# Second softmax of batches 2 to 7: eight TensorE transposes replaced by VectorE block transposes and sixteen small DMAs

## The chip, the cores and the metric

The kernel runs on one core of a Trainium2 chip. The metric is the device time of one execution in microseconds (us). TensorE is called PE below, the loading of its weights PEld, VectorE DVE, ScalarE ACT and SyncE SP; SPq and ACTq are the queues on which SP and ACT issue DMAs.

## The reference, cut to what matters

```python
# x: 8 batches x 8 heads x 512 tokens x 64;  state: 8 x 8 x 32 x 64
scores = scale * x @ state.T;   a  = softmax(scores);   xread = a @ state
scores2 = scale * state @ x.T;  a2 = softmax(scores2);  sread = a2 @ x      # the part that is changed
attn = concat([xread, sread], axis=2)          # 512 + 32 rows per head
h = attn_as_rows(4352 x 512) @ w_in            # 512 -> 2048
g = where(h >= 1, h, where(h <= -1, 0, (h + 1)**2 / 4))
out = g @ w_out                                # 2048 -> 512
```

## The kernel before

All large products are made of three TensorE products of split numbers (high times high, low times high, high times low). The hidden layer of one batch is done in 8 steps j = 0 to 7. In each step `g1(b, j)` makes two hidden tiles in PSUM (L481 to L483, 12 matmuls), which ACT and DVE turn into `gh` and `gl` (`relu` L487, `square` L490, `bound` L493, `high` L502, `low` L507), and `g2` of the step before multiplies those of the previous step with w_out (L539 to L541, 24 matmuls). `bound` reads the hidden tiles last, so the next `g1` needs it: the PSUM tag `h` has two buffers.

The attention of batch b+1 is spread over the steps of batch b. A generator, `Attention.steps`, is advanced after steps 1, 3, 4 and 6, and `sw_make` (L423, L438, L442) prepares weights after steps 0, 2, 4 and 6. The four pieces of the generator are:

- after step 1: the scores `sc` (L253); DVE turns them in 32x32 blocks for the first softmax (L260) and finds the maxima for the second (L318); ACT takes the second softmax's exponentials to `e2` (L322, `exp2`).
- after step 3: the first softmax's sums and scaling, and `turn2` and `keep_turned`: eight 128x128 TensorE transposes of `e2` into the PSUM tile `e2p` (L333), one ACT copy back over `e2` (L337), and the reciprocal `r2` (L339, L340).
- after step 4: the first softmax turned back (L300) and split (L303, L306), and `read2`: 32 small products `sr` with `e2` as weights and the tokens `xn` (L353).
- after step 6: `keep2`, a transpose of the result.

Batches 0 and 1 are written in an order made by a planner (`Plan`, which has its own calls of `turn2` and `keep_turned`); batches 2 to 7 take theirs from `steps`. In that second part a scheduler of the framework orders the instructions of each engine by its own priorities and places the semaphore waits. A DMA counts on one of eight semaphores in turn (DMAHW0 to DMAHW7 in the listings); a DMA waits until the one eight before it has landed. The loads of `xt` and `xn` for the next batches stand on SPq too (L217, L222).

Of the kernel before, what the change touches and what calls it, by code (L numbers as in the profile page):

```python
# [8 lines left out]
F32 = mybir.dt.float32  # L9
# [128 lines left out]
def state_exchange_moe(  # L138
# [17 lines left out]
    nc = tc.nc  # L156
    B, P, NT, H, D = x.shape
    S = NT * P
    NS = 32
    DM = H * D  # L160
    NPR = H // 2
# [9 lines left out]
    small = ctx.enter_context(tc.tile_pool(name="small", bufs=1))  # L171
    const = ctx.enter_context(tc.tile_pool(name="const", bufs=1))
    work = ctx.enter_context(tc.tile_pool(name="work", bufs=2))
# [7 lines left out]
    def ps_h(name):  # L181
        return ps.tile([P, 512], F32, tag="h", bufs=2, name=name)

    def ps_mm(name):
        return ps.tile([P, 2, 512], F32, tag="mm", bufs=1, name=name)
# [39 lines left out]
    class Attention:  # L225
# [109 lines left out]
        def keep_turned(self):  # L335
# [3 lines left out]
            nc.vector.tensor_scalar_add(self.r2, self.sum2, 1e-9)  # L339
            nc.vector.reciprocal(out=self.r2, in_=self.r2)  # L340

        def read2(self):
            b = self.b
            xn = loaded.pop(("xn", b))
            if b < 2:
                sr = self.sr = ps_mm(f"sr{b}")
            else:
                sr = self.sr = ps_h(f"sr{b}").rearrange("p (q f) -> p q f", q=2)
            for q in range(2):
                for t in range(NT):  # L350
                    for pr in range(NPR):
                        c0 = t * P + pr * NS
                        nc.tensor.matmul(  # L353
                            sr[pr * NS:(pr + 1) * NS, q, :D], lhsT=self.e2[:, q, c0:c0 + NS],
                            rhs=xn[:, t, 2 * pr + q], start=t == 0, stop=t == NT - 1,
                        )
# [22 lines left out]
        def steps(self):  # L379
            self.scores()  # L380
            for q in range(2):
                self.turn(q)
            for q in range(2):
                self.top2(q)
            for q in range(2):
                self.exp2(q)
            yield
            for f in (self.top1, self.less1, self.exp1, self.sum1, self.inv1, self.norm1):
                for q in range(2):
                    f(q)  # L390
            self.turn2()
            self.keep_turned()
            yield
            for q in range(2):
                self.back(q)
                self.high1(q)
                self.rest(q)
            self.read2()
            self.scale2()
            yield  # L400
            self.keep2()
            self.keep()
            yield
# [406 lines left out]
    for i, (b, j) in enumerate(steps):  # L810
        if j == 0:
            if b + 1 < B:
                loaded["xt", b + 1] = load_xt(b + 1)
                loaded["xn", b + 1] = load_xn(b + 1)
                att = Attention(b + 1).steps()
            elif b == B:
                sh, sl = (work.tile([P, NPR, B * NS], F32R, tag=t, name=f"s{t}") for t in ("ath", "atl"))
                src = srT.rearrange("p a b n -> p a (b n)")
                nc.vector.tensor_copy(sh, src)
                nc.vector.tensor_tensor(out=sl, in0=src, in1=sh.bitcast(F32), op=ALU.subtract)  # L820
                att_of[B] = (sh, sl)
        g1(b, j)
        if i + 1 < len(steps):
            splits(*steps[i + 1])
        g2(*(steps[i - 1] if i else (0, NJ - 1)))
        between_steps(b, j)
# [44 lines left out]
```

## Time and profile before

| | |
|---|---|
| runs | 666.66, 666.80 and 666.98 us, median 666.8 |
| profiled execution | span 664.4 us from the first to the last instruction; what lies around it is the other 2.4 us of the runs (no separate time of this execution is listed) |
| granted TensorE clock | 0.997 of full speed over the span |
| busy share of PE, ACT, DVE | 98%, 55%, 51% |
| one batch | 73.8 us: the scores of batch 3 start at 188.74 us, those of batch 4 at 262.55 us |

A busy PE is the union of pipelined matmuls, so the distance from the start of one matmul to the start of the next is the price of one, not its own duration: 0.227 us for the 128x512 matmuls, though each lasts 0.39 us. "Idle before" in a row is the time its engine stood still ahead of it, with the instruction that ended the wait.

### The profile page before, as it was taken

How to read it: one execution, taken by the hardware profiler on the slowest of the kernel's cores; microseconds unless marked ns; L12 is line 12 of the kernel's file. 1: busy time of each engine (PE TensorE's matmuls, PEld its weight loads, DVE VectorE, ACT ScalarE, POOL GpSimd, SP SyncE). 2: the span in 40 equal slices, each digit the busy share in tenths (PEclk: the TensorE clock that was granted, in tenths of full speed). 3: DMA queues.
4: the chain of work that ended last, by engine and by line, in shares of the span. 5: the costliest groups of instructions: out<-in, count | busy, mean ns of one | idle time of the engine just before them, and what ended most of it. 6: DMA issues, size and time to landing. Idle time of an engine off the chain costs nothing.

```text
span 664.4 us, 10294 instructions
## 1 busy us (share of the span) xinstructions
PE 653.2 (98%) x4444; PEld 515.3 (78%) x4444; DVE 339.9 (51%) x489; ACT 362.8 (55%) x462; POOL 0.8 (0%) x7
## 2 busy tenths in 40 slices
PE   6999999999999999999999999999999999999997
PEld 6777777777778777777777877777778787778895
DVE  4999953933365334833375335733384343333431
ACT  4899845644556445644555444644555455454632
POOL 0000000000000000000000000000000000000000
PEclk9899999999999999999999999999999999999999
DMA  8896101110110102110110103010100001000101
GB/s 346 350 393 273 64 1 64 63 65 0 65 64 1 64 1 78 50 65 1 64 64 1 64 1 120 7 64 1 65 1 1 1 26 39 1 1 1 63 1 32
DMA packets 11085, 43.64 MB, mean 66 GB/s; under 512 B 1312, under 2 KB 1440, under 8 KB 7968
## 3 DMA queue, kind: packets, MB, share of 16 engines
q1 hardware_dynamic: 5952, 33.75, 13.3%
q10 hardware_dynamic: 5088, 9.24, 3.7%
q8 instruction: 34, 0.56, 0.3%
q14 instruction: 11, 0.09, 0.0%
HBM read 34.08 MB, written 8.91 MB: 65 GB/s over the span
## 4 chain that ended last, share of the span: by engine, by line
PE 92%; ACT 4%; DVE 2%; DMA 1%; issue 0%; ACTq 0%; SPq 0%
PE acc L539 18%; PE acc L541 18%; PE acc L540 18%; PE h L481 11%; PE h L482 9%; PE h L483 9%; PE sw L423 5%; DMA xt<-in_xt_dram 1%; PE sr L353 1%; PE sc L253 1%; PE e2p L333 1%; PE warmed L198 1%; ACT u L487 1%; ACT raw_i L593 1%; ACT gh L502 0%; ACT raw_o L593 0%
## 5 line engine op out<-in xcount | busy, mean ns | idle before, releaser
L539 PE MATMUL acc<-wo,gh 128*128 128x512 f32 x544 | 213.3, 392 | 0.0
L541 PE MATMUL acc<-wo,gl 128*128 128x512 f32 x544 | 211.8, 389 | 0.0
L540 PE MATMUL acc<-wo,gh 128*128 128x512 f32 x544 | 211.7, 389 | 0.0
L493 DVE SCALAR_TENSOR_TENSOR u<-u,h 128x512 f32<-128x512 f32 x136 | 87.4, 683 | 170.5 <-ACT u L490 170.2
L487 ACT ACTIVATE u<-h,half 128x512 f32<-128x512 f32 x136 | 93.7, 690 | 146.5 <-PE h L483 145.8
L539 PEld LDWEIGHTS acc<-wo,gh 128*128 128x128 f32 x544 | 102.2, 188 | 24.6 <-issue 3.7
L541 PEld LDWEIGHTS acc<-wo,gl 128*128 128x128 f32 x544 | 102.1, 188 | 21.6
L540 PEld LDWEIGHTS acc<-wo,gh 128*128 128x128 f32 x544 | 102.2, 188 | 20.8
L507 DVE TENSOR_TENSOR gl<-u,gh 128x1024 fp32r<-128x1024 f32 x68 | 83.2, 1223 | 60.8 <-ACT gh L502 60.8
L502 ACT CAST gh<-u 128x1024 fp32r<-128x1024 f32 x68 | 71.5, 1052 | 67.0 <-DVE u L493 67.0
L490 ACT ACTIVATE u<-u 128x1024 f32<-128x1024 f32 x68 | 72.3, 1064 | 1.6
L423 PE MATMUL sw<-w,sb 64*32 64x256 f32 x1024 | 35.9, 383 | 2.2 <-DVE w L601 2.2
L423 PEld LDWEIGHTS sw<-w,sb 64*32 64x32 f32 x1024 | 15.1, 106 | 18.2 <-issue 11.3
L554 ACT COPY o<-acc 128x512 f32<-128x512 f32 x33 | 18.9, 583 | 12.0 <-PE acc L541 12.0
L481 PE MATMUL h<-ath,sw_4h 128*128 128x512 f32 x60 | 25.3, 422 | 0.1
L481 PE MATMUL h<-ath,sw_2h 128*128 128x512 f32 x60 | 24.9, 415 | 0.0
L481 PE MATMUL h<-ath,sw_0h 128*128 128x512 f32 x60 | 24.4, 410 | 0.0
L481 PE MATMUL h<-ath,sw_6h 128*128 128x512 f32 x60 | 23.9, 398 | 0.0
L483 PE MATMUL h<-atl,sw_4h 128*128 128x512 f32 x60 | 23.5, 392 | 0.0
L482 PE MATMUL h<-ath,sw_4l 128*128 128x512 f32 x60 | 23.5, 391 | 0.0
L483 PE MATMUL h<-atl,sw_6h 128*128 128x512 f32 x60 | 23.5, 391 | 0.0
L482 PE MATMUL h<-ath,sw_0l 128*128 128x512 f32 x60 | 23.5, 391 | 0.0
(173 smaller groups left out, 733.3 us busy)
## 6 DMA issues: line engine op xcount, KB each, us to landing
raw_i<-in_moe_w_in_dram SPq DMA_DIRECT2D x8, 1024.0 KB, 6.5
raw_o<-in_moe_w_out_dram SPq DMA_DIRECT2D x8, 1024.0 KB, 8.6
xn<-in_x_dram SPq DMA_DIRECT2D x8, 1024.0 KB, 4.7
out_dram<-o ACTq DMA_DIRECT2D x32, 256.0 KB, 2.0
xt<-in_xt_dram SPq DMA_DIRECT2D x15, 512.0 KB, 4.5
xt<-in_xt_dram ACTq DMA_DIRECT2D x1, 512.0 KB, 7.8
sb<-in_state_dram SPq DMA_DIRECT2D x1, 448.0 KB, 12.0
out_dram<-o SPq DMA_DIRECT2D x4, 64.0 KB, 1.7
```

The lines of the kernel that those rows point to most:

```text
L423: nc.tensor.matmul(pt[pr * NS:(pr + 1) * NS, hh, i * CI:(i + 1) * CI], lhsT=sb[rows, b, pr], rhs=w32[c + i][rows, pr], start=True, stop=True,)
L481: nc.tensor.matmul(o, lhsT=wh[:, k, sl], rhs=ah[:, k], start=first, stop=False)
L482: nc.tensor.matmul(o, lhsT=wl[:, k, sl], rhs=ah[:, k], start=False, stop=False)
L483: nc.tensor.matmul(o, lhsT=wh[:, k, sl], rhs=al[:, k], start=False, stop=last)
L487: nc.scalar.activation(out=self.u[:, i], in_=self.hs[i], func=AF.Relu, scale=0.5, bias=half)
L490: nc.scalar.activation(out=self.u, in_=self.u, func=AF.Square)
L493: nc.vector.scalar_tensor_tensor(out=self.u[:, i], in0=self.u[:, i], scalar=1.0, in1=self.hs[i], op0=ALU.min, op1=ALU.max,)
L502: nc.scalar.copy(out=gh, in_=self.u)
L507: nc.vector.tensor_tensor(out=gl, in0=self.u, in1=gh.bitcast(F32), op=ALU.subtract)
L539: nc.tensor.matmul(a, lhsT=lh, rhs=oh, start=f == 0, stop=False)
L540: nc.tensor.matmul(a, lhsT=lh, rhs=ol, start=False, stop=False)
L541: nc.tensor.matmul(a, lhsT=ll, rhs=oh, start=False, stop=f == NF - 1)
```

## The change

In `steps`, which rules batches 2 to 7, the two calls `turn2` and `keep_turned` after step 3 are gone. After step 1, behind `exp2`, two calls of `turn_blocks` make DVE transpose `e2` in 32x32 blocks into a new SBUF tile `eb`, and `shuffle` issues sixteen DMAs on SPq that put the blocks where the 128x128 transposes would have put them, back in `e2`. Each DMA moves a block of 32 partitions x 8 runs of 32 numbers (128 bytes a run, 32 KB in all). `eb` takes one of the two buffers of the tag `tmp`, in turn with `zt`. `r2` is computed in `shuffle`.

```diff
+        def turn_blocks(self, q):
+            if q == 0:
+                self.blocks = work.tile([P, 2, S], F32, tag="tmp", name=f"eb{self.b}")
+            nc.vector.transpose(out=self.blocks[:, q], in_=self.e2[:, q])
+
+        def shuffle(self):
+            b = self.b
+            self.r2 = small.tile([P, 2], F32, tag="r2", name=f"r2_{b}")
+            nc.vector.tensor_scalar_add(self.r2, self.sum2, 1e-9)
+            nc.vector.reciprocal(out=self.r2, in_=self.r2)
+            src, dst = (
+                v.rearrange("p q (t r n) -> p (q t) r n", r=NPR, n=NS) for v in (self.blocks, self.e2)
+            )
+            for r in range(NPR):
+                for pr in range(NPR):
+                    nc.sync.dma_start(
+                        out=dst[r * NS:(r + 1) * NS, :, pr], in_=src[pr * NS:(pr + 1) * NS, :, r]
+                    )
+
@@ steps
             for q in range(2):
                 self.exp2(q)
+            for q in range(2):
+                self.turn_blocks(q)
+            self.shuffle()
             yield
             for f in (self.top1, self.less1, self.exp1, self.sum1, self.inv1, self.norm1):
                 for q in range(2):
                     f(q)
-            self.turn2()
-            self.keep_turned()
             yield
```

The new lines stand ahead of most of the kernel, so a line of before from L342 on is 19 or 20 higher after: `read2`'s L353 becomes L372, `bound`'s L493 becomes L513. In the listings a number behind a name is the batch, and for `h`, `u`, `gl`, `gh` and `sw` the batch and the step.

TensorE, at the end of step 3 in the loop of batch 2 (attention of batch 3), before:

```order
L541 MATMUL acc2_3_1663<-wo2_482,gl2_2_1732 128x512
L333 MATMUL e2p3_1842<-ident_73,e2_3_1702 128x128 [waits DVE_49]
L333 MATMUL e2p3_1842<-ident_73,e2_3_1702 128x128 x7
L481 MATMUL h2_4_0_1856<-ath2_973,sw2_4h_1776 128x512 [waits DVE_49]
L482 MATMUL h2_4_0_1856<-ath2_973,sw2_4l_1777 128x512
```

and after:

```order
L560 MATMUL acc2_3_1672<-wo2_482,gh2_2_1762 128x512
L561 MATMUL acc2_3_1672<-wo2_482,gl2_2_1763 128x512
L501 MATMUL h2_4_0_1874<-ath2_973,sw2_4h_1807 128x512 [waits DVE_49]
L502 MATMUL h2_4_0_1874<-ath2_973,sw2_4l_1808 128x512
L503 MATMUL h2_4_0_1874<-atl2_974,sw2_4h_1807 128x512
```

The eight transposes are gone and the hidden products of step 4 follow `g2` directly. One step later, at `read2`, the piece before is

```order
L423 MATMUL sw2_6_1903<-w32_6_93,sb_85 32x256 x7
L423 MATMUL sw2_6_1903<-w32_7_94,sb_85 32x256 x8
L353 MATMUL sr3_1931<-xn3_1554,e2_3_1702 32x64 [waits DMAHW1_49,DVE_49]
L353 MATMUL sr3_1931<-xn3_1554,e2_3_1702 32x64 x31
L481 MATMUL h2_5_0_1967<-ath2_973,sw2_4h_1776 128x512 [waits DVE_49]
```

and after

```order
L443 MATMUL sw2_6_1921<-w32_7_94,sb_85 32x256 x8
L372 MATMUL sr3_1949<-xn3_1563,e2_3_1711 32x64 [waits DMAHW1_49,DMAHW4_49,DMAHW0_49,DVE_49]
L372 MATMUL sr3_1949<-xn3_1563,e2_3_1711 32x64 [waits DMAHW5_49,DMAHW1_49]
L372 MATMUL sr3_1949<-xn3_1563,e2_3_1711 32x64 [waits DMAHW6_49,DMAHW2_49]
L372 MATMUL sr3_1949<-xn3_1563,e2_3_1711 32x64 [waits DMAHW7_49,DMAHW3_49]
L372 MATMUL sr3_1949<-xn3_1563,e2_3_1711 32x64 x28
L501 MATMUL h2_5_0_1985<-ath2_973,sw2_4h_1807 128x512 [waits DVE_49]
```

so `read2` now waits for all eight DMA semaphores, spread over its first four products, and everything behind it on TensorE waits with it.

VectorE, after step 1 in the same loop, before:

```order
L271 TENSOR_REDUCE m1_3_1690<-z3_1689 128x16
L275 TENSOR_TENSOR z3_1689<-z3_1689,m1_3_1690 128x512 [waits DVE_49] x2
L339 TENSOR_SCALAR r2_3_1852<-sum2_3_1704 128x2 [waits Activation_49]
L340 RECIPROCAL r2_3_1852<-r2_3_1852 128x2 [waits DVE_49]
L493 SCALAR_TENSOR_TENSOR u2_2_1711<-u2_2_1711,h2_2_0_1712 128x512 [waits Activation_49]
L493 SCALAR_TENSOR_TENSOR u2_2_1711<-u2_2_1711,h2_2_1_1720 128x512
L284 TENSOR_REDUCE s1_3_1691<-z3_1689 128x16 [waits Activation_49] x2
L507 TENSOR_TENSOR gl2_2_1732<-u2_2_1711,gh2_2_1731 128x1024 [waits Activation_49]
```

and after:

```order
L271 TENSOR_REDUCE m1_3_1699<-z3_1698 128x16
L275 TENSOR_TENSOR z3_1698<-z3_1698,m1_3_1699 128x512 [waits DVE_49]
L345 STREAM_TRANSPOSE eb3_1720<-e2_3_1711 128x512 [waits Activation_49] x2
L350 TENSOR_SCALAR r2_3_1723<-sum2_3_1713 128x2
L513 SCALAR_TENSOR_TENSOR u2_2_1742<-u2_2_1742,h2_2_0_1743 128x512 [waits Activation_49]
L351 RECIPROCAL r2_3_1723<-r2_3_1723 128x2 [waits DVE_49]
L513 SCALAR_TENSOR_TENSOR u2_2_1742<-u2_2_1742,h2_2_1_1751 128x512
L275 TENSOR_TENSOR z3_1698<-z3_1698,m1_3_1699 128x512
L284 TENSOR_REDUCE s1_3_1700<-z3_1698 128x16 [waits Activation_49]
L527 TENSOR_TENSOR gl2_2_1763<-u2_2_1742,gh2_2_1762 128x1024 [waits Activation_49]
```

Both block transposes, which wait for ACT's `exp2`, stand ahead of `bound` of step 2 now, and one of the two subtractions (L275) has moved behind it.

SyncE's queue around the same place, before:

```order
L222 DMA xn3_1554<-in_x_dram 128x2048 [waits DMAHW2_49,PE_49]
L217 DMA xt4_2134<-in_xt_dram 128x1024 [waits DMAHW6_49,DMAHW7_49,DMAHW0_49,PE_49]
L217 DMA xt4_2134<-in_xt_dram 128x1024
L222 DMA xn4_2137<-in_x_dram 128x2048 [waits DMAHW1_49,PE_49]
L217 DMA xt5_2717<-in_xt_dram 128x1024 [waits DMAHW6_49,DMAHW7_49,DMAHW5_49,PE_49]
```

and after, to the tenth of the sixteen new DMAs:

```order
L217 DMA xt4_2152<-in_xt_dram 128x1024 [waits DMAHW6_49,PE_49]
L217 DMA xt4_2152<-in_xt_dram 128x1024 [waits DMAHW7_49]
L357 DMA e2_3_1711<-eb3_1720 32x8x32 [waits DMAHW3_49,DMAHW4_49,DMAHW2_49,DMAHW5_49,DMAHW0_49,DVE_49]
L357 DMA e2_3_1711<-eb3_1720 32x8x32 [waits DMAHW1_49]
L357 DMA e2_3_1711<-eb3_1720 32x8x32 [waits DMAHW2_49]
L357 DMA e2_3_1711<-eb3_1720 32x8x32 [waits DMAHW3_49]
L357 DMA e2_3_1711<-eb3_1720 32x8x32 [waits DMAHW4_49]
L357 DMA e2_3_1711<-eb3_1720 32x8x32 [waits DMAHW5_49]
L357 DMA e2_3_1711<-eb3_1720 32x8x32 [waits DMAHW6_49]
L357 DMA e2_3_1711<-eb3_1720 32x8x32 [waits DMAHW7_49]
L357 DMA e2_3_1711<-eb3_1720 32x8x32 [waits DMAHW0_49]
L357 DMA e2_3_1711<-eb3_1720 32x8x32 [waits DMAHW1_49]
```

The sixteen stand behind the load of `xt` and ahead of that of `xn`, which waits for `read2` in both versions; from the ninth on each waits for the one eight places ahead of it.

## The prediction

> **What bounds the kernel now.** I read the page's busy shares first, then the chain that ended last. The first two fields of an engine's row are its busy us and share of the span.
>
> ```profile
> span 664.4 us, 10294 instructions
> PE 653.2 (98%) x4444; PEld 515.3 (78%) x4444; DVE 339.9 (51%) x489; ACT 362.8 (55%) x462; POOL 0.8 (0%) x7
> ...
> PE 92%; ACT 4%; DVE 2%; DMA 1%; issue 0%; ACTq 0%; SPq 0%
> ```
>
> PE is busy for 653.2 of 664.4 us, and the chain is PE for 92%. So what leaves PE's instruction stream in batches 2 to 7 is time won, unless something else comes late there; what DVE, ACT or a queue gains or loses counts only where PE has to wait for it. Whether PE stands still at the changed place is in the timeline (start us, duration us, engine, line): the transposes of batch 3 with the matmuls around them, then a passage from `g2` to `g1` with nothing between, and the first and last of the six groups.
>
> ```profile
> 202.03 0.39 PE L539 MATMUL acc<-wo,gh 128*128 128x512 f32 x1
> ...
> 207.25 0.39 PE L541 MATMUL acc<-wo,gl 128*128 128x512 f32 x1
> 207.48 1.03 PE L333 MATMUL e2p<-ident,e 128*128 128x128 f32 x8
> 208.27 0.48 PE L481 MATMUL h<-ath,sw_4h 128*128 128x512 f32 x1
> 208.59 0.40 PE L482 MATMUL h<-ath,sw_4l 128*128 128x512 f32 x1
> ...
> 165.64 0.39 PE L539 MATMUL acc<-wo,gh 128*128 128x512 f32 x1
> ...
> 171.08 0.39 PE L481 MATMUL h<-ath,sw_0h 128*128 128x512 f32 x1
> 171.31 0.39 PE L482 MATMUL h<-ath,sw_0l 128*128 128x512 f32 x1
> ...
> 133.62 1.03 PE L333 MATMUL e2p<-ident,e 128*128 128x128 f32 x8
> ...
> 502.87 1.03 PE L333 MATMUL e2p<-ident,e 128*128 128x128 f32 x8
> ```
>
> PE does not wait: the transposes start 0.23 us after the last matmul, the usual distance.
>
> **The change part by part.** *Eight transposes leave PE, six times.* From the first matmul of `g2` to the second of the following `g1` it is 208.59 - 202.03 = 6.56 us with the transposes, and 171.31 - 165.64 = 5.67 us without. The difference, 0.89 us, holds the transposes and the slower start of the matmul behind them. Six batches: 5.3 us. Nothing lies beside this on PE, so all of it is on the path.
>
> *Two DVE block transposes and the moved `r2`.* The same operation on the same size stands in the groups (busy us, mean ns); the places where it can hurt are in the timelines of DVE, ACT and PE:
>
> ```profile
> L300 DVE STREAM_TRANSPOSE zt<-z 128x512 f32<-128x512 f32 x16 | 11.3, 704 | 0.0
> ...
> 194.65 0.21 ACT L322 ACTIVATION_READ_ACCUMULATOR e<-sc,nm 128x1 f32 x1
> 193.65 1.28 DVE L275 TENSOR_TENSOR z<-z,m 128x512 f32<-128x512 f32 x2
> 195.83 1.28 DVE L493 SCALAR_TENSOR_TENSOR u<-u,h 128x512 f32<-128x512 f32 x2 [0.58 <-ACT u L490]
> 204.21 1.28 DVE L493 SCALAR_TENSOR_TENSOR u<-u,h 128x512 f32<-128x512 f32 x2
> 199.18 0.50 PE L481 MATMUL h<-ath,sw_2h 128*128 128x512 f32 x1
> ```
>
> Two of 704 ns are 1.41 us. The new order takes half of the 1.28 us of L275 (0.64) from ahead of `bound` and `bound` had 0.58 us of idle ahead of it, so it moves by 0.2 us (1.41 - 0.64 - 0.58), and by 1.41 us at the worst. It ends at 197.11 (195.83 + 1.28); the next `g1`, which needs the PSUM buffers, starts at 199.18: 2.07 us of cover. One step later `bound` ends at 205.49, and `g1` would start at 208.27 - 0.79 = 207.48 without the transposes: 1.99 us of cover for 1.41 us of added DVE work. I cost it at nothing; with that cover gone each further us of DVE work would be a us of PE, six times. Next late would be `gl`, which `g2` needs later than `g1` needs `bound`.
>
> *ACT loses the copy of the turned block, and the PSUM tag `mm` one user.*
>
> ```profile
> 208.55 1.01 ACT L337 COPY e<-e2p 128x1024 f32<-128x1024 f32 x1 [1.92 <-PE e2p L333]
> ```
>
> It ended at 209.56; the products that need it (L353) and the next user of `mm` came 7 to 8 us later, so its end was waited for by nobody: nothing.
>
> *Extra waits at `read2`.* It has one more semaphore instruction ahead of its first product and three among the next three. Its present one lasts 51 ns:
>
> ```profile
> L353 PEldq EVENT_SEMAPHORE  x8: 51/51/51, 31.4 to 512.1; - x8
> ```
>
> Ends: 0, if PE's queue runs ahead of the array as it does at other waits, and 4 x 51 ns = 0.2 us a batch, 1.2 us in all; a gain is excluded, since waits are only added. I take a quarter, 0.3 us, since three of the four lie behind the first product, but the queue is ahead there.
>
> *Sixteen DMAs.* They can start when the second block transpose ends: `exp2` ends at 194.86 (194.65 + 0.21) and DVE's first L275 at 194.3, so at 194.86 + 0.70 = 195.6. `read2` needs them:
>
> ```profile
> 217.64 1.10 PE L353 MATMUL sr<-xn,e 128*32 128x64 f32 x64
> ```
>
> Less the 0.89 us won, that is 216.75. The window is 21.2 us. The trace has no SBUF-to-SBUF copy and no 128-byte packet; the nearest rows are issue times on SPq, the landing of the 64 KB stores (the last field of an issue group, in us), and the DMA shares of two stages: 174 to 178 us with one store in 2 KB packets and 440 to 448 us with one load in 8 KB packets (128 of data and 16 small ones in each; packets, MB, share of 16 engines):
>
> ```profile
> 0.74 0.39 SPq L217 DMA_DIRECT2D xt<-in_xt_dram  x1
> 1.19 0.90 SPq L573 DMA_DIRECT2D raw_i<-in_moe_w_in_dram  x2
> 2.12 0.45 SPq L573 DMA_DIRECT2D raw_o<-in_moe_w_out_dram  x1
> 2.61 0.59 SPq L739 DMA_DIRECT2D sb<-in_state_dram  x1
> ...
> raw_i<-in_moe_w_in_dram SPq DMA_DIRECT2D x8, 1024.0 KB, 6.5
> ...
> out_dram<-o ACTq DMA_DIRECT2D x4, 64.0 KB, 2.0
> ...
> q10 hardware_dynamic: 144, 0.26, 16.9%
> ...
> q1 hardware_dynamic: 144, 1.05, 37.1%
> ```
>
> Issue: 16 x 0.39 to 0.59 = 6.2 to 9.4 us, and 2.0 us for the last to land. The engines: each of the 16 DMAs has 256 runs, 4096 in all, 256 for each of 16 engines. The stages were 4 and 8 us long: 0.169 x 4 x 16 / 128 = 84 ns for a 2 KB packet, 0.371 x 8 x 16 / 128 = 371 ns for 8 KB. Upper end: a 128-byte run costs as much as 2 KB, 256 x 84 = 21.6 us. Lower end: it costs by its bytes, 84/16 = 5 ns, 1.4 us. The 8 KB packet costs 4.4 times the 2 KB one, so cost follows bytes; still I give half of the 84 ns to a fixed part: 45 ns, 11.5 us. So the DMAs take 8 to 11 us by issue and 13.5 us by engines with landing; the largest end, 21.6 + 2.0 = 23.6 us, is 2.4 us over the window. I take 13.5 us: hidden, with over 7 us to spare. `xn` behind them on SPq waits for `read2` anyway; the load of `xt` ahead of them is issued at 189.93 and PE doesn't feel it, as the distance of its matmuls beside it shows:
>
> ```profile
> 189.93 0.80 SPq L217 DMA_DIRECT2D xt<-in_xt_dram  x2
> ...
> 192.63 0.39 PE L539 MATMUL acc<-wo,gh 128*128 128x512 f32 x1
> ...
> 197.39 0.39 PE L539 MATMUL acc<-wo,gh 128*128 128x512 f32 x1
> ```
>
> (197.39 - 192.63) / 21 = 0.227 us, the same as without a transfer (207.25 - 202.03 over 23). So I cost the new transfers' traffic at nothing for PE as well.
>
> *Sum.* 664.4 - 5.3 + 0.3 = 659.4 us of span; the median of the runs, 666.8, lies 2.4 us above that span: 661.8 us, 0.75% less.
>
> **The rivals.** *The DMAs come late (slower).* One mechanism: SPq does not keep several small DMAs in flight, so that each costs a whole landing. 16 x 2.0 = 32 us is 10.8 us over the window, six times: 666.8 - 5.3 + 65 = 726 us. It decides from 21.2 us on; at 22.1 us the gain is gone. For it: the engines' upper end reaches 23.6 us (666.8 - 5.3 + 6 x 2.4 = 676 us), and from the ninth on each DMA waits for an earlier one. Against it: four loads are issued from 0.74 to 2.6 us while one takes 6.5 us to land, so several are in flight, and eight semaphores allow eight. The Trainium skill, "DMA: Bandwidth & Descriptors", section "Rules for kernel authors", says to join many small transfers into one, as below 64 KB mostly overhead is paid; its section on the anatomy of a DMA puts that at about 2.0 us each. By that rule, paid one after another, it would be an estimate of 33 us (16 x 2.07). The trace's 64 KB landing of 2.0 us agrees with the size of the overhead, and its loads in flight together speak against paying it sixteen times. Chance 0.13.
>
> *DVE becomes late.* If the two transposes and what they push back cost `bound` 3 us at one of the two places instead of 1.41, PE waits about 1 us a batch: 666.8 - 5.3 + 6 = 667.5 us, no change. Against it: 2 us of cover at both. Chance 0.05.
>
> *The gain is eaten by waits at `read2`* (DMAs of 21.7 to 22.1 us, or semaphores that cost several times 51 ns): 664.5 to 666.8 us. Only a narrow band of costs gives it. Chance 0.04.
>
> **How the numbers follow.** The forecast, 661.8 us, has 0.78. Its own range: 661.5 with free semaphores, 662.7 with full ones; down to 660.8, for what a spacing of 0.227 us leaves open six times (half of one each, 0.7 us), and up to 664.5 for a short wait at `read2`, to where the third rival begins. That leaves out the three rivals, 0.22 together, so the range goes on to 665.0, a part of the third. 0.2% of 666.8 us, 1.3 us, is about what can be told from no change. Faster (under 665.5): the forecast and half of the third rival, 0.80. The same: most of the DVE case and the rest of the third, 0.06. Slower: the late DMAs and a little of the DVE case, 0.14.
>
> **What would show it.** Right: no TensorE transposes after batch 1; `g1` of step 4 0.227 us behind `g2`; the last DMA of each group landed by about 13 us after the block transposes; no wait of PE at `read2`; DVE busy some 8 us longer (12 x 0.7), ACT 6 us shorter. Wrong: PE idle ahead of `read2` released by a DMA, with the landing time telling whether issue, engines or waits on SPq set it; or PE idle ahead of `g1` released by `bound`. The price most open is the one of a 128-byte run.

## The result, and the profile after

The changed kernel is faster. The first timing gave a median of 661.3 us against 666.7, a ratio of 0.9914 (95% interval 0.9899 to 0.993). One of its four runs, the profiled one, was a slow one of 804.76 us at a granted clock of 0.754, which the ratio leaves out (the median of the other three is 661.13 us). Beside the experiments the kernel was timed twice more: 659.8 us against 666.74 (0.9891, 0.9876 to 0.9906) and 660.14 us against 666.34 (0.9903, 0.9886 to 0.9919). That is 5.4 to 6.9 us less; 661.8 us was forecast, 5.0 less. The two later medians lie below the low end of the forecast's own range, 660.8 us. In the timing with 6.9 us, three of the four runs of the changed kernel had a granted clock of 1.000 and most runs beside it 0.996 or 0.997, so a part of that gain may be the clock's. All views of "after" below are of the last timing's profiled run (660.0 us), whose granted clock, 0.997, is that of the profile before.

The page of after: span, busy shares, and the chain that ended last.

```profile
span 658.2 us, 10359 instructions
PE 648.4 (99%) x4396; PEld 510.4 (78%) x4396; DVE 345.6 (52%) x501; ACT 356.2 (54%) x456; POOL 0.8 (0%) x7
...
PE 91%; ACT 3%; DVE 2%; issue 0%; DMA 0%; SPq 0%; ACTq 0%
```

PE is still the bound: 48 matmuls fewer, 4.8 us less busy. DVE is 5.7 us busier (345.6 - 339.9; some 8 was forecast) and ACT 6.6 us less (362.8 - 356.2). The groups of after, by line:

```profile
L345 DVE STREAM_TRANSPOSE eb<-e 128x512 f32<-128x512 f32 x12 | 8.1, 708 | 0.0
...
L333 PE MATMUL e2p<-ident,e 128*128 128x128 f32 x16 | 2.2, 280 | 1.4 <-DVE sw_1l L462 1.4
L337 ACT COPY e<-e2p 128x1024 f32<-128x1024 f32 x2 | 2.1, 1042 | 0.0
```

Sixteen TensorE transposes and two ACT copies are left, those of batches 0 and 1. What a batch saves is read from one landmark, the score products of each batch, in the chain of after and then of before (start, us, engine, line); the last row of each is the last copy to the output tile `o`:

```profile
114.66 1.02 PE sc L253 x16
...
479.43 1.02 PE sc L253 x16
...
654.22 0.69 DVE o L572
```

```profile
114.95 1.02 PE sc L253 x16
...
484.20 1.02 PE sc L253 x16
...
659.86 0.68 DVE o L552
```

Five periods lie between: (479.43 - 114.66) / 5 = 72.95 us after, (484.20 - 114.95) / 5 = 73.85 us before. A batch is 0.90 us shorter; 0.89 was forecast. The spans differ by 6.2 us: 6 x 0.90 = 5.4, another 0.29 that stood already at the first landmark (114.95 - 114.66), and some 0.5 left, which lies behind the last copy to `o`: from there to the end of the span it is 4.5 us before (664.4 - 659.86) and 4.0 us after (658.2 - 654.22).

The changed place in after's timelines, batch 3: DVE's block transposes and the two halves of `bound` (L513), SPq's DMAs, and PE. Behind the arrow is what ended an engine's idle time.

```profile
193.08 1.35 DVE L345 STREAM_TRANSPOSE eb<-e 128x512 f32<-128x512 f32 x2
194.67 0.69 DVE L513 SCALAR_TENSOR_TENSOR u<-u,h 128x512 f32<-128x512 f32 x1 [0.19 <-ACT u L510]
195.35 0.67 DVE L513 SCALAR_TENSOR_TENSOR u<-u,h 128x512 f32<-128x512 f32 x1
```

```profile
194.46 11.06 SPq L357 DMA_DIRECT2D e<-eb  x16
216.75 0.34 SPq L222 DMA_DIRECT2D xn<-in_x_dram  x1
```

```profile
198.02 0.50 PE L501 MATMUL h<-ath,sw_2h 128*128 128x512 f32 x1
...
206.09 0.39 PE L561 MATMUL acc<-wo,gl 128*128 128x512 f32 x1
206.31 0.39 PE L501 MATMUL h<-ath,sw_4h 128*128 128x512 f32 x1
...
214.56 1.09 PE L443 MATMUL sw<-w,sb 64*32 64x256 f32 x32
215.59 1.10 PE L372 MATMUL sr<-xn,e 128*32 128x64 f32 x64
216.62 0.50 PE L501 MATMUL h<-ath,sw_4h 128*128 128x512 f32 x1
```

Where the transposes stood, `g1` of step 4 now follows `g2` by 0.22 us. The window from the second block transpose (194.43) to `read2` (215.59) is 21.2 us, as forecast. The DMAs fill 11.06 us of it by their issue alone (10.5 to 11.6 us in the six batches). By the lines of after, their issue times (min/median/max, ns) and landing, and the semaphore instructions at `read2`:

```profile
L357 SPq DMA_DIRECT2D e<-eb x96: 586/609/1482, 121.5 to 496.4; - x96
...
DMA to landing us min/median/max: 1.9/1.9/3.7
```

```profile
L372 PEldq EVENT_SEMAPHORE  x32: 51/51/51, 31.2 to 507.1; - x32
```

The landing counts from the start of an issue. The last issue takes 0.60 us, so it starts at 194.46 + 11.06 - 0.60 = 204.92, and its DMA lands 1.9 us later, at 206.8 us: 12.4 us behind the block transposes, 8.8 us ahead of `read2`. How busy the DMA engines are meanwhile stands in the DMA view of 196 to 205 us:

```profile
q1 hardware_dynamic: 3539, 0.43, 29.2%
```

3539 packets of 128 bytes take 0.292 x 9 us x 16 engines = 42 us, so 11.9 ns each. The engines stand idle for 70% of the time: the issue on SPq sets the duration.

### The profile page after: what moved, and what is told of

It is laid out like the page before. It is cut to its first block, busy times and chain, and to the rows that moved or that the text cites. A ratio compares the mean times of both kernels' runs of the same rounds, so it can differ in the third digit from the quotient of the medians.

```text
span 803.0 us, 10359 instructions
## 1 busy us (share of the span) xinstructions
PE 795.8 (99%) x4396; PEld 546.0 (68%) x4396; DVE 348.6 (43%) x501; ACT 358.5 (45%) x456; POOL 0.8 (0%) x7
## 4 chain that ended last, share of the span: by engine, by line
PE 96%; DVE 1%; ACT 0%; issue 0%
PE acc L561 20%; PE acc L560 19%; PE acc L559 19%; PE h L503 11%; PE h L501 10%; PE h L502 10%; PE sw L443 5%; PE sr L372 1%; PE sc L253 1%; PE e2p L333 0%; PE rt L389 0%; DVE wo L632 0%; DVE wf L621 0%; DVE w L621 0%; ACT wo L628 0%; DVE o L572 0%
## 5 line engine op out<-in xcount | busy, mean ns | idle before, releaser
L561 PE MATMUL acc<-wo,gl 128*128 128x512 f32 x544 | 253.5, 466 | 0.0
L559 PE MATMUL acc<-wo,gh 128*128 128x512 f32 x544 | 251.6, 463 | 0.0
L560 PE MATMUL acc<-wo,gh 128*128 128x512 f32 x544 | 243.5, 448 | 0.0
L513 DVE SCALAR_TENSOR_TENSOR u<-u,h 128x512 f32<-128x512 f32 x136 | 87.8, 683 | 230.8 <-ACT u L510 230.8
L560 PEld LDWEIGHTS acc<-wo,gh 128*128 128x128 f32 x544 | 115.3, 212 | 43.8
L559 PEld LDWEIGHTS acc<-wo,gh 128*128 128x128 f32 x544 | 107.1, 197 | 49.0 <-issue 3.8
L443 PE MATMUL sw<-w,sb 64*32 64x256 f32 x1024 | 43.2, 454 | 0.7 <-DVE w L621 0.7
L501 PE MATMUL h<-ath,sw_2h 128*128 128x512 f32 x60 | 28.6, 477 | 0.0
L503 PE MATMUL h<-atl,sw_2h 128*128 128x512 f32 x60 | 28.4, 474 | 0.0
L503 PE MATMUL h<-atl,sw_4h 128*128 128x512 f32 x60 | 28.4, 473 | 0.0
L501 PE MATMUL h<-ath,sw_0h 128*128 128x512 f32 x60 | 28.3, 476 | 0.0
L503 PE MATMUL h<-atl,sw_0h 128*128 128x512 f32 x60 | 27.4, 456 | 0.0
L503 PE MATMUL h<-atl,sw_6h 128*128 128x512 f32 x60 | 27.3, 455 | 0.0
## 6 DMA issues: line engine op xcount, KB each, us to landing
sb<-in_state_dram SPq DMA_DIRECT2D x1, 448.0 KB, 11.6
```

The costliest lines, as they stand in the source:

```text
L443: nc.tensor.matmul(pt[pr * NS:(pr + 1) * NS, hh, i * CI:(i + 1) * CI], lhsT=sb[rows, b, pr], rhs=w32[c + i][rows, pr], start=True, stop=True,)
L501: nc.tensor.matmul(o, lhsT=wh[:, k, sl], rhs=ah[:, k], start=first, stop=False)
L503: nc.tensor.matmul(o, lhsT=wh[:, k, sl], rhs=al[:, k], start=False, stop=last)
L513: nc.vector.scalar_tensor_tensor(out=self.u[:, i], in0=self.u[:, i], scalar=1.0, in1=self.hs[i], op0=ALU.min, op1=ALU.max,)
L559: nc.tensor.matmul(a, lhsT=lh, rhs=oh, start=f == 0, stop=False)
L560: nc.tensor.matmul(a, lhsT=lh, rhs=ol, start=False, stop=False)
```

## The experiments

**What the replacement costs: leave it out.** `turn_blocks` and `shuffle` go, `r2` stays.

```diff
-            for q in range(2):
-                self.turn_blocks(q)
-            self.shuffle()
+            self.r2 = small.tile([P, 2], F32, tag="r2", name=f"r2_{self.b}")
+            nc.vector.tensor_scalar_add(self.r2, self.sum2, 1e-9)
+            nc.vector.reciprocal(out=self.r2, in_=self.r2)
```

> The changed kernel without the block transposes and without the DMAs; the TensorE transposes stay away too, so the second softmax's exponentials of batches 2 to 7 are used unturned (the turning is left out). What is left is the bare price of the TensorE turning. Theory (DVE's, the DMAs' and the semaphores' costs are all hidden): 661.0 to 661.4 us, within 0.3 us of the changed kernel. Rival (the replacement costs something on the path): 660.5 us or less, and the difference to the changed kernel is what the replacement costs.

660.84 us (660.38 to 661.65), with the changed kernel at 659.8 (658.98 to 660.09) beside it; their ratios to before, 0.991 (0.9895 to 0.9925) and 0.9891 (0.9876 to 0.9906), overlap. It is 1.0 us above the changed kernel, not within 0.3 us as expected, at granted clocks of 0.996 to 0.999, where three of the other's four runs had 1.000. So the times show only that it isn't below the changed kernel. The landmark in its chain shows more: (479.61 - 114.89) / 5 = 72.94 us a batch, as against 72.95 with the replacement. Nothing of the replacement is on the path. The waits at `read2` in particular: from `sw` to the `h` behind `read2` it is 2.06 us in after (216.62 - 214.56, with the added semaphores) and 2.05 us here.

```profile
114.89 1.02 PE sc L253 x16
...
479.61 1.02 PE sc L253 x16
```

```profile
214.73 1.09 PE L443 MATMUL sw<-w,sb 64*32 64x256 f32 x32
...
216.78 0.50 PE L501 MATMUL h<-ath,sw_4h 128*128 128x512 f32 x1
```

**The changed kernel once more**, with the same runs of before.

> The changed kernel once more, for a profile at full clock. Theory (the transposes' 0.89 us a batch is saved in full, six times, and nothing else reaches the path): 661.3 us, no wait of PE at `read2`, the sixteen DMAs issued 0.61 us apart and the last landed some 12.5 us after the second block transpose, with about 8 us to spare. Rival (a part of the gain is eaten by the extra waits or by DVE): a gap ahead of the products of `read2` or of `g1` of 0.1 us or more, six times.

659.8 us, 1.5 us less than expected. In this run too PE never waits at `read2` or at `g1` of batches 2 to 7, and an issue takes 0.61 us, as in the rows of after above.

**The reverse: add the work to the kernel before.** The DMAs write into `spare`, a tile that takes the room of the unused `pad`.

```diff
-    pad = small.tile([P, PAD], F32, name="pad")
...
+    spare = const.tile([P, 2, S // 2], F32, name="spare")
...
+            for q in range(2):
+                self.turn_blocks(q)
+            self.shuffle()
             yield
```

> The kernel before, its TensorE transposes kept, plus the two DVE block transposes and sixteen DMAs of the same runs per batch, into a tile that nobody reads. Theory (the added work is all beside PE): 666.7 us, as before, within 0.3 us. Rival (its traffic or DVE's time slows PE): 667.3 us or more, 0.1 us a batch and up.

666.18 us (664.49 to 667.64, 11 runs) against 666.74; ratio 0.9988 (0.9976 to 1.0). The time shows no cost. The landmark in its chain:

```profile
116.25 1.02 PE sc L252 x16
...
485.63 1.02 PE sc L252 x16
```

(485.63 - 116.25) / 5 = 73.88 us a batch, 0.03 us more than before. Together: leaving the eight transposes out is the whole gain, and the other half of the change costs 0.03 us a batch at most in these executions, in both directions.

**How long the DMAs take, 1: ask for the result one step earlier.**

```diff
+            self.read2()
+            self.scale2()
+            yield
...
-            if j in (1, 3, 4, 6):
+            if j in (1, 2, 3, 4, 6):
```

> The changed kernel with `read2` and its scaling one step earlier, in a piece of their own behind step 2; all is computed. PE reaches the products of `read2` of batch 3 at about 200.2 us (the place where step 2's first products now end), the DMAs end at about 195.6 + 16 x 0.61 + 1.9 = 207.3 to 208.0 us. Theory (the issue on SPq, 0.61 us each, and one landing set the duration): PE waits some 7 us a batch for the last DMA, six times, 42 us: 703 us, between 690 and 715, and the wait is released by a DMA. Rival 1 (only the packets on the sixteen engines count, 256 of about 12 ns each, 3.1 us, + 1.9 us of landing): the DMAs end at 200.6 us, no wait, 661 us. Rival 2 (each DMA costs a landing of its own, 1.9 us): 30 us, PE waits 25 us a batch, 810 us.

702.4 us (694.2 to 703.4), ratio 1.0505 (1.0455 to 1.0555). The number came out as the theory had it, but not by its way. The waits of PE (us in total, times, longest) in the profiled run, the fastest of the four (span 692.5 us):

```profile
PE sw L444 <- DVE sw_6l L463: 17.6, 6, 2.9
PE h L502 <- DVE rs L380: 2.4, 6, 0.4
...
PE sr L372 <- DMA e<-eb: 1.6, 3, 0.7
```

Most of what can be named is a wait of the next `sw` product for `sw_6l`, 2.9 us a batch: the scheduler had also pulled other products ahead, so PE came to `read2` later than assumed, just when the DMAs landed. The three rows come to 21.6 of the 34.3 us by which the span is longer than after's (692.5 - 658.2); PE is also 12.7 us longer busy (661.1 - 648.4), for which I have no cause. The three runs at 702 to 703 us had a granted clock of 0.977 to 0.981, against 0.993 in the profiled one, so a part of the median may be the clock's. The time of this run therefore doesn't speak for the theory. One passage of its chain does, since here the chain ran through the DMAs: SPq's issues one after another, the thirteenth landing, and then PE's products.

```profile
358.23 0.56 SPq L357
358.84 0.60 SPq L357
...
366.51 0.61 SPq L357
367.17 1.90 DMA e<-eb
```

```profile
369.11 0.30 PE L372 MATMUL sr<-xn,e 128*32 128x64 f32 x2 [0.58 <-DMA e<-eb]
```

Issues start 0.61 to 0.66 us apart, but for one of 1.80, one landing of 1.90 us follows the start of the last that is needed (367.17 + 1.90 = 369.07), and PE goes on at 369.11. Each DMA paying for a landing of its own (rival 2) is out, and so is a duration set by packets alone (rival 1).

**How long, 2: twice the DMAs, the same bytes.**

```diff
+            for q in range(2):
+                t = slice(q * NT, (q + 1) * NT)
...
-                        out=dst[r * NS:(r + 1) * NS, :, pr], in_=src[pr * NS:(pr + 1) * NS, :, r]
+                        out=dst[r * NS:(r + 1) * NS, t, pr], in_=src[pr * NS:(pr + 1) * NS, t, r]
```

> The changed kernel with each DMA cut into two, one for each head half q: 32 DMAs of 128 runs a batch instead of 16 of 256, the same bytes and the same order on TensorE; all is computed. In the profile of the changed kernel the group of batch 3 starts at 193.45 us and `read2` at 214.57 us. Theory A (the issue has a price per run, about 2.4 ns, as 256 runs take 0.61 us): 0.33 us each, 32 x 0.33 = 10.6 us, landed 1.9 us later at about 206 us: no wait, 659.5 to 661.5 us. Rival B (0.61 to 0.65 us per DMA, whatever its runs): 32 x 0.65 = 20.8 us, landed at about 216.2 us: PE waits 1 to 1.6 us ahead of `read2`, six times: 666 to 671 us.

662.78 us (661.8 to 663.96), ratio 0.9945 (0.9928 to 0.9962). The issues, and batch 3 on SPq and PE:

```profile
L359 SPq DMA_DIRECT2D e<-eb x192: 585/599/1547, 121.0 to 509.0; - x192
```

```profile
194.13 21.46 SPq L359 DMA_DIRECT2D e<-eb  x32
```

```profile
215.91 1.65 PE L374 MATMUL sr<-xn,e 128*32 128x64 f32 x64
217.49 0.50 PE L503 MATMUL h<-ath,sw_4h 128*128 128x512 f32 x1
```

With half the runs a DMA still takes 599 ns to issue: my theory of a price per run is wrong, the price is per DMA, as rival B had it. The group's last issue, a long one of 1.47 us, starts at 214.12 and lands 2.7 us later, at 216.8, when `read2` has been at work since 215.91: from its first product to the `h` behind it takes 1.58 us (217.49 - 215.91) instead of 1.03 (216.62 - 215.59). The cost is smaller than B's 1 to 1.6 us a batch, 0.5 us by the spans ((661.2 - 658.2) / 6), since the products of the first head half need only the first sixteen DMAs and run before: in batch 3 the first 32 of the 64 have started by 216.4. This kernel stands a little past the point from which the DMAs show.

**How long, 3: sixteen more DMAs of one run each, ahead of the shuffle.**

```diff
+            for i in range(16):
+                nc.sync.dma_start(out=pad[i:i + 1, :32], in_=self.blocks[i:i + 1, 1, :32])
```

> The changed kernel with sixteen more DMAs a batch ahead of the shuffle on SPq, each of one run of 128 bytes into the unread `pad` tile; the order on TensorE is the same. Theory (the issue is a price per DMA, and what sets it is the kind of access, 0.6 us in and out of SBUF against 0.33 us for the loads): 0.6 us each, the group with the shuffle is 32 issues in about 21 us, as when the DMAs were cut in two, and PE waits ahead of `read2`: 662 to 665 us. Rival (a DMA of one run is cheaper, as little as the loads or less): 0.3 us each or under, the group takes 15.5 us or less, no wait, 660 to 661 us.

668.5 us (one run; before 666.34 beside it).

```profile
196.17 10.05 SPq L356 DMA_DIRECT2D pad<-eb  x16
206.32 10.50 SPq L359 DMA_DIRECT2D e<-eb  x16
```

```profile
L356 SPq DMA_DIRECT2D pad<-eb x96: 497/587/1477, 121.9 to 503.7; - x96
```

```profile
218.53 1.45 PE L374 MATMUL sr<-xn,e 128*32 128x64 f32 x62 [0.94 <-DMA e<-eb]
```

A single run of 128 bytes takes 587 ns to issue, where a load of 1 MB takes 0.34 us (`xn` above). The issues fill 20.65 us (206.32 + 10.50 - 196.17); the last starts at 216.2 and lands 2.6 us later, 22.6 us behind the start of the group. PE waits for the DMAs, and the kernel is slower than before: (666.7 - 658.2) / 6 = 1.4 us a batch, more than the 0.9 us won. The expected 662 to 665 us was too little, as here all products wait for the late group. The forecast's first rival, DMAs that come late, is a real danger: it begins where the group takes longer than the window of 21.2 us, and 32 issues do; the change has 16.

**How much cover DVE has: do the block transposes two, three and four times.** The diff is that of twice.

```diff
-            nc.vector.transpose(out=self.blocks[:, q], in_=self.e2[:, q])
+            for _ in range(2):
+                nc.vector.transpose(out=self.blocks[:, q], in_=self.e2[:, q])
```

> The changed kernel with every block transpose done twice over (the second writes the same values): 1.41 us more of DVE work a batch at the same place, the same order on TensorE. Theory (there is cover: `bound` would end at 195.76 and 196.42 us in batch 3, and `g1` needs its buffers at 197.01 us and 1.4 us later): no cost, within 0.7 us of the changed kernel, 659.5 to 661.5 us. Rival (DVE's time has no cover): each added us is a us of PE, 6 x 1.41 = 8.5 us, 668 to 670 us.

> The changed kernel with every block transpose done three times: 2.82 us more of DVE work a batch. Theory: the cover of 2.0 to 2.7 us is just used up: `bound` ends at 197.2 us where `g1` would start at 197.01 us, and `gl` at 200.2 us where the third matmul of `g2` would start at about 200.2 us; PE waits 0.2 to 0.6 us a batch, 1 to 4 us in all: 661 to 665 us, and the wait is released by DVE at L513 or L527's lines. Rival 1 (no cover at all): 17 us, 677 us. Rival 2 (more cover than worked out): no cost, 660 to 661.5 us.

> The changed kernel with every block transpose done four times, 1.24 us more DVE work a batch than with three, where `bound` ended 0.6 us ahead of the `g1` that needs its buffer. Theory (the cover ends between three and four): PE waits 0.7 us a batch for `bound` and as much again for `gl`, behind which one more operation has moved on DVE: 4 to 10 us, 664 to 670 us, with waits of PE on DVE in the records. Rival (another wait than `bound` or `gl` binds, and the cover goes on): within 1 us of the changed kernel.

Twice 660.19 us (659.27 to 660.7), three times 659.97 (659.46 to 660.82), four times 664.16 (663.8 to 664.67). The first two cost nothing, three times against my expectation. DVE and PE in batch 3, three times:

```profile
193.06 3.73 DVE L346 STREAM_TRANSPOSE eb<-e 128x512 f32<-128x512 f32 x6
196.75 0.68 DVE L514 SCALAR_TENSOR_TENSOR u<-u,h 128x512 f32<-128x512 f32 x1
```

```profile
198.00 0.50 PE L502 MATMUL h<-ath,sw_2h 128*128 128x512 f32 x1
```

and four times:

```profile
194.28 4.91 DVE L346 STREAM_TRANSPOSE eb<-e 128x512 f32<-128x512 f32 x8
199.15 0.68 DVE L514 SCALAR_TENSOR_TENSOR u<-u,h 128x512 f32<-128x512 f32 x1
```

```profile
199.88 0.50 PE L502 MATMUL h<-ath,sw_2h 128*128 128x512 f32 x1 [0.59 <-DVE u L514]
```

The waits of PE in this run (us in total, times, longest):

```profile
PE h L502 <- DVE u L514: 3.6, 6, 0.6
```

`g1`'s first product needs the first half of `bound` only: with four, PE goes on at 199.88, right behind its end at 199.83 (199.15 + 0.68). That one ends at 195.36 in after, 2.66 us ahead of 198.02; with three at 197.43, 0.57 us ahead. The fourth adds 1.18 us (4.91 - 3.73): 0.6 us too late, and PE waits 0.59 us at each of the six places, 3.6 us. Measured against after, 664.16 - 660.14 = 4.0 us. I had taken too little cover for the third one, and 0.70 us for each transpose where those in a row take 0.60 to 0.62 (3.73 / 6, 4.91 / 8). The wait for `gl` that I expected with four did not come.

**Further: batch 1 by DVE and DMA too.** In the plan of the first stage, batch 1's TensorE turning and its copy give way to the block transposes on DVE and the shuffle on SP.

```diff
+        if b:
...
+                op(("eb", b, q), "DVE", 0.62, m("turn_blocks", q), [("exp2", b, q)] + [("eb", b, 0)] * q, take=take)
+            read(("turned", b), 10.4, m("shuffle"), after=[("eb", b, 0), ("eb", b, 1)])
...
-        4: lambda: tensor(("e2p", 1), 0.9, lambda: atts[1].turn2(), [("exp2", 1, 0), ("exp2", 1, 1)],
-                          take=[("mm", ("e2p", 1))]),
```

> The changed kernel with batch 1 turned in the same way (batch 0 keeps TensorE). The first 75 us are planned from a table of costs, so other instructions there change place as well. Theory (one more group of eight transposes leaves PE, 0.89 us): 0.9 us less than the changed kernel, 659 to 660.5 us. Rival (DVE has no idle time in that stage, where it also joins the weights, and the DMAs queue between weight loads on SPq): the 1.41 us of DVE push the products back, 0.5 to 3 us more than the changed kernel, 661 to 664 us.

658.7 us (658.35 to 660.88), ratio 0.9892 (0.9874 to 0.9909), without the changed kernel beside it. So both were timed on one chip:

> The changed kernel, on the same chip and beside the same runs as the one with batch 1 turned as well: 659.5 to 661.5 us. It is the yardstick for that one.

> Batch 1 turned by DVE and DMA as well, now beside the changed kernel on one chip. Theory (another 0.89 us leaves PE and nothing else comes late): 0.5 to 1.5 us under the changed kernel. Rival (its first run was chance, and the planned stage gives the 0.89 us back in other waits): within 0.4 us of it.

659.09 us (658.34 to 659.62) against 660.14 (659.57 to 660.48): 1.05 us less, where 0.89 was to be won. Its ratio to before is 0.9887 (0.9872 to 0.9902), after's 0.9903 (0.9886 to 0.9919); these overlap, so 1 us is likely, not certain. The gain has to stand ahead of the first landmark, which is at 113.57 us here (114.56 in the first run) and at 114.66 in the changed kernel; but runs of kernels with the changed kernel's first stage have it anywhere from 113.7 to 114.9, so the traces don't show it. No wait for DVE or a DMA took its place, though the group now follows the last weight loads on SPq and its issues take 12.3 us.

```profile
55.21 12.30 SPq L357 DMA_DIRECT2D e<-eb  x16
```

Against before it is the fastest of the kernels timed that compute all, 7.3 us less (666.34 - 659.09).

## Why the prediction was right, step by step

- *Eight transposes leave PE, 0.89 us, six times.* Right: 0.90 us a batch, and leaving out the replacement as well gains nothing more (72.94 us a batch against 72.95).
- *Two DVE transposes at no cost.* Right, and the cover was larger than worked out. I measured it to the end of the second half of `bound` (2.07 us); the first half is what `g1` waits for (2.66 us), and the DVE rival needs three further pairs before it shows. `bound` did not even move by the 0.2 us worked out: it starts 7.02 us behind the batch's scores in both kernels (195.83 - 188.81 before, 194.67 - 187.65 after).
- *ACT's copy at nothing.* ACT lost 6.6 us of work and the time did not follow: nothing beyond the 0.90 us a batch.
- *Extra waits at `read2`, 0.3 us of 0 to 1.2.* They cost nothing: the passage from `sw` to the `h` behind `read2` takes 2.05 to 2.06 us in each of the six batches, with the added semaphores and without. So the 51 ns of each are spent while PE's queue is ahead. Without this term the sum is 661.5 us.
- *Sixteen DMAs hidden, 13.5 us.* 12.4 us came out, but the parts were mis-sized and the errors partly cancelled. The engines, which I let bind, took 11.9 ns for a 128-byte run instead of the 45 ns taken: 256 runs in 3.0 us, not 11.5, nearer the lower end that I gave (5 ns, cost by bytes) than the upper (84). The issue took 10.5 to 11.6 us, over my 6.2 to 9.4, because I let the DMAs cost what loads from DRAM cost. And I set a whole landing behind the end of the last issue, where it counts from its start, 0.6 us too much. So issue binds; the landing stayed at 1.9 us in the median, so neither the engines nor waits on SPq do.
- *The DMAs come late.* The mechanism as I wrote it, a whole landing per DMA, is refuted by the spacing of 0.61 to 0.66 us. The threshold held: the kernel with sixteen added DMAs of one run needs 22.6 us, 1.4 us over the window of 21.2 us, and loses 1.4 us a batch, more than the gain. The Trainium skill, "DMA: Bandwidth & Descriptors", section "Rules for kernel authors", counsels against many small transfers, as they pay mostly overhead. That holds in kind: 587 ns of issue for 128 bytes. Yet the overhead that is paid one after another is the issue, and the landing overlaps. The 2.0 us for each that the prediction takes from the Trainium skill, "DMA: Bandwidth & Descriptors", section "Anatomy of one DMA", stand there for DMAs that GpSimd issues. Those here are issued by SP and land in 1.9 us by the trace.
- *Traffic beside PE's matmuls.* At nothing, and the kernel with the added work shows it so (0.9988; 0.03 us a batch).

What I had no term for: some 0.8 us of the 6.2 between the two spans lies outside the batches, 0.29 ahead of the first landmark and 0.5 behind the last copy to `o`. The change is not its cause as far as the runs show: the kernel without the replacement has batches as short, but its first landmark at 114.89 us and 4.5 us behind the last copy, like the kernel before. Single runs of one kernel differ by about as much. So the forecast was right in what the change does, 5.3 us forecast and 5.4 found; what the runs gained beyond that (up to 6.9 us) is not shown to come from it.

## What to carry to other kernels

When one engine is the bound, work moved to others is worth what it took on the bound engine as long as every hand-over meets its due time; so look for the due time of each new product (here 21 us for the DMAs, 2.7 us for DVE) and compare. The chain of small DMAs on one queue lasted here (count - 1) x the spacing of issues + one landing, 15 x 0.65 + 1.9 = 11.7 us, and in the six batches up to 1.2 us more where an issue was held up: count the DMAs first, and bytes and runs after. A time that comes out as predicted is no proof: the moved `read2` hit its 703 us by other waits, which only the list of waits told.

## What the hardware showed that was not expected

- Issuing a DMA from SBUF to SBUF on SPq takes 0.6 us whether it has 256 runs (609 ns), 128 (599) or one (587), against 0.33 to 0.43 us (medians) for the 1 MB loads. What makes the difference isn't shown: the load of `sb`, from DRAM, took 0.59 us before and 0.55 after. The Trainium skill, "DMA: Bandwidth & Descriptors", section "Issuing engines are not separate DMA queues", calls the time to initiate a DMA usually small relative to the DMA; here it is a third of the 1.9 us that one needs to land, and in a row of sixteen the last issue starts 10.5 us behind the first, of 12.4 us in all.
- In most groups of 16 one issue takes 0.9 to 1.8 us instead of 0.6, and during each of these an instruction fetch is under way (the queues q8 and q14 of the profile). In eleven profiled runs with such groups 43 of 1280 issues take more than 0.8 us, and all 43 fall on a fetch; of the other 1237 only 98 do. The fetch is therefore the likely cause, but no run tests it. One case, from the kernel with `read2` moved, is the issue in its chain and the fetch in its DMA view of 360.6 to 362.6 us, where the one packet is on its engine for 0.046 x 2.0 us x 16 = 1.5 us:

```profile
360.79 1.76 SPq L357
```

```profile
q8 instruction: 1, 0.02, 4.6%
```

- A 128-byte packet from SBUF to SBUF takes 11.9 ns of a DMA engine, a seventh of the 84 ns of a 2 KB packet of a store.
